# Three of nine score blocks of every pair are copied, negated, from PSUM to SBUF by the pass that takes their row maximum

## The chip, the cores and the metric

One program on one core of a Trainium2 chip. The metric is device time in microseconds. Three runs of the kernel before took 596.67 to 598.54 us, with a median of 598.43 us. The profile comes from one more execution, which took 597.25 us in all and spans 594.6 us from its first to its last instruction.

## The reference

The kernel computes an attention with a threshold on the scores, and passes its output through a soft mixture of experts. All is fp32.

```python
scores = scale * np.matmul(q, k.transpose(0, 1, 3, 2))      # 8 batches, 8 heads, 576 x 576, head size 64
thresh = np.max(scores, axis=-1, keepdims=True) - tau
scores = np.where(scores >= thresh, scores, -1000000000.0)
scores = scores - np.max(scores, axis=-1, keepdims=True)
attn = np.exp(scores)
attn = attn / (np.sum(attn, axis=-1, keepdims=True) + 1e-09)
x = np.matmul(attn, v)                                       # laid out as 4608 tokens x 512
...
logits = x @ phi                                             # 32 slots, 4 for each of 8 experts
# softmax over tokens (d) and over slots (c)
slot_input = d.T @ x
h = np.maximum(slot_input[e] @ w1[e], 0.0)
slot_out[e] = h @ w2[e]
out = c @ slot_out
```

For a row of scores only three things are needed: its maximum, the exponentials of the scores less the maximum, and the sum of those whose score reaches the maximum less tau.

## The kernel before

**Pairs and blocks.** Two heads of a batch make a pair; there are 32 pairs, four to a batch. The 2 x 576 rows of scores of a pair are nine blocks of 128 rows by 576 keys (`i` = 0 to 8 in `pair`): four from each head, and a ninth that holds the last 64 rows of both heads (its probabilities are the buffer `pL`, those of the others lie two by two in four buffers `p2`).

**The steps of a block.** TensorE (PE) computes the scores into a PSUM region `s` (L500, for the ninth block L505). VectorE (DVE) takes the negated row maximum, `nmx` (L510). ScalarE (ACT) writes exp(s + nmx) to SBUF (L518). GpSimd (POOL) makes the threshold `thr` = -nmx - |tau| (L521). DVE reads the scores a second time, compares them with `thr`, multiplies the result onto the exponentials and sums the row into `r` (L524): the masked sum. After every two blocks POOL adds 1e-9 to the sums (L531), DVE takes the reciprocals (L534), and POOL scales the two blocks (L538). PE transposes them through PSUM (L425), ACT copies the transposes to SBUF (L430), and PE multiplies them with the values (L585, twice a pair: AVa and AVb). At the end of a batch, `dispatch` updates the mixture's running softmax.

**Four PSUM regions.** All of PSUM is cut into four regions of two banks. A score block takes one whole region, from its matmul until both its readers, the exp and the masked sum, are done. The same four regions serve the transposes, the products with the values and the small work of `dispatch`.

**What sets the order.** `G.add` only records an operation with an engine, a duration in ns for the planner, a due time, and what it reads and writes. `Order.plan` then lays all operations of the attention part out in one go: each engine takes, whenever it is free in the planner's own clock, the due operation with the lowest number for which buffers can be had. The due times come from `TABLE`, one number for each operation of the first pair, of every middle pair, of the last pair, and of the ends of batches. On the chip each engine then runs its list strictly in that order.

**Weights.** The 64 units of expert weights (512 KB each) go to SBUF: 28 (`NPRE`) during the attention part into slots of their own, 19 (`NHOST`) into the space that the last pairs of the attention leave, and 17 into slots that the first expert products have used up. After the last pair come the expert products (L880, L914) and the combination with the output (L954 to L974).

Of the kernel before, what the change touches and what calls it, by code (L numbers as in the profile page):

```python
# [1054 lines left out]
```

## Time and profile before

| What | us |
|---|---|
| Median of three runs | 598.43 |
| The profiled execution, in all | 597.25 |
| Its span | 594.6 |
| Steady rhythm of the pairs, from | about 23 |
| Two batches (eight pairs and their two ends), steady | 126.83 |
| One pair, steady | 14.97 |
| Last product of the attention part with the values, end | about 520 |
| Expert products, last end | about 563 |

The granted clock of TensorE is 1.00 in all stretches up to 580 us. The profile has a page with totals of each engine, groups of instructions by line, a view of the waits, a chain of the work that ended last, a timeline of each engine, and windows that give each engine's busy time in a stretch. A duration in these views is that of the instruction by itself; DVE starts the next a little before the last ends, so the cost of one in a row of them is read from the distance of two starts in the timeline.

### The profile page before, as it was taken

Reading aid. Unit: us, or ns where it says so; the run is one execution under the profiler, and the core shown is the slowest. Engines: PE = TensorE matmul, PEld = TensorE weight load, DVE = VectorE, ACT = ScalarE, POOL = GpSimd, SP = SyncE. Lnnn points to the kernel's source line nnn. Section 1 sums busy time; section 2 is a strip of 40 time slices with the busy share of each in tenths; the row PEclk is TensorE's granted clock in tenths of the full one; section 3 lists DMA queues with packets and bytes.
Section 4 is the critical chain, followed back from the end, with each engine's and each line's share of the span. In section 5 each row is a group of like instructions: output and inputs, shape, how many; then the busy total and the mean of one; then the engine's idle time right before and its main releaser. Section 6 shows DMA issues by size and latency. Waiting matters only on the chain.

```text
span 594.6 us, 17473 instructions
## 1 busy us (share of the span) xinstructions
PE 544.4 (92%) x6404; PEld 333.5 (56%) x6404; DVE 484.1 (81%) x1146; ACT 442.8 (74%) x753; POOL 348.9 (59%) x799
## 2 busy tenths in 40 slices
PE   8799999999999999999999999999999998999991
PEld 6455555555555555555565555555565555553471
DVE  5999998999898998999889989998989999431182
ACT  3788887888888887888878888888788887622071
POOL 2877776577676775677657765776667755511030
PEclk9999999999999999999999999999999999999996
DMA  7255555355543554533333332333223322699578
GB/s 164 66 154 153 156 154 153 86 156 154 153 132 115 154 154 133 154 83 84 83 84 84 84 84 70 81 81 82 56 70 83 81 64 60 239 361 408 233 309 325
DMA packets 31988, 82.97 MB, mean 140 GB/s; under 512 B 4640, under 2 KB 12832, under 8 KB 31904
## 3 DMA queue, kind: packets, MB, share of 16 engines
q1 hardware_dynamic: 31904, 81.87, 45.7%
q8 instruction: 50, 0.82, 0.6%
q14 instruction: 34, 0.28, 0.2%
HBM read 72.42 MB, written 9.44 MB: 138 GB/s over the span
## 4 chain that ended last, share of the span: by engine, by line
PE 54%; ACT 20%; DVE 9%; issue 8%; POOL 5%; DMA 1%; DVEq 0%; POOLq 0%; ACTq 0%
PE ps L585 22%; PE ps L500 10%; PE ps L425 10%; ACT p L518 6%; ACT pTb L430 5%; DVE p L524 4%; ACT pTa L430 4%; POOL p L538 3%; ACT pTl L430 3%; PE h L880 3%; DVE nmx L510 2%; PE so L914 2%; ACT pTl L570 1%; PE ps L720 1%; PE ps L417 1%
## 5 line engine op out<-in xcount | busy, mean ns | idle before, releaser
L510 DVE TENSOR_REDUCE nmx<-ps 128x1 f32<-128x576 f32 x288 | 205.5, 752 | 30.3 <-PE ps L500 26.7
L518 ACT ACTIVATE p<-ps,nmx 128x576 f32<-128x576 f32 x256 | 183.5, 746 | 29.4 <-DVE nmx L510 25.2
L538 POOL TENSOR_SCALAR p<-p,ri 128x576 f32<-128x576 f32 x256 | 188.1, 742 | 24.2 <-PE ps L500 13.5
L524 DVE SCALAR_TENSOR_TENSOR p<-ps,thr,p 128x576 f32<-128x576 f32 x256 | 199.7, 811 | 2.9 <-POOL thr L521 2.7
L500 PE MATMUL ps<-k,q 64*128 64x288 f32 x1024 | 168.7, 432 | 2.9 <-DVE p L524 1.5
L425 PE MATMUL ps<-ident,p 64*128 64x64 f32 x2304 | 105.9, 227 | 24.2 <-POOL thr L521 10.3
L425 PEld LDWEIGHTS ps<-ident,p 64*128 64x128 f32 x2304 | 88.3, 138 | 55.1 <-POOL thr L521 14.1
L500 PEld LDWEIGHTS ps<-k,q 64*128 64x128 f32 x1024 | 84.5, 187 | 36.6 <-ACT pTb L430 11.8
L521 POOL TENSOR_SCALAR thr<-nmx,nabs 128x1 f32<-128x1 f32 x288 | 75.1, 264 | 37.2 <-DVE nmx L510 27.5
L531 POOL TENSOR_SCALAR ri<-r 128x2 f32<-128x2 f32 (+1 forms) x160 | 30.6, 192 | 95.9 <-DVE p L524 41.8
L430 ACT COPY pTb<-ps 128x1024 f32<-128x1024 f32 (+1 forms) x95 | 80.7, 878 | 2.0 <-PE ps L425 0.9
L585 PE MATMUL ps<-pTb,vv 128*64 128x320 f32 x512 | 75.9, 438 | 1.3
L430 ACT COPY pTa<-ps 128x1024 f32<-128x1024 f32 x64 | 65.4, 1024 | 8.6 <-PE ps L425 7.7
L585 PE MATMUL ps<-pTa,vv 128*64 128x256 f32 x512 | 62.3, 385 | 0.0
L430 ACT COPY xT<-ps 128x256 f32<-128x256 f32 (+1 forms) x63 | 25.1, 399 | 46.7 <-PE ps L585 46.7
L585 PEld LDWEIGHTS ps<-pTb,vv 128*64 128x64 f32 x512 | 34.0, 136 | 39.0 <-ACT pTb L430 13.6
L585 PEld LDWEIGHTS ps<-pTa,vv 128*64 128x64 f32 x512 | 33.9, 136 | 25.8 <-ACT pTa L430 11.5
L585 PE MATMUL ps<-pTl,vv 128*64 128x256 f32 (+1 forms) x256 | 41.9, 406 | 0.0
L534 DVE RECIPROCAL ri<-ri 128x2 f32<-128x2 f32 (+1 forms) x160 | 25.9, 162 | 14.2 <-POOL ri L531 14.1
L845 POOL TENSOR_TENSOR c<-lall,crow 128x512 f32<-128x512 f32 x9 | 9.3, 1043 | 44.1 <-PE ct L417 39.1
L430 ACT COPY pTl<-ps 128x256 f32<-128x256 f32 x64 | 23.7, 370 | 6.2 <-PE ps L425 5.6
L524 DVE SCALAR_TENSOR_TENSOR pL<-ps,thr,pL 128x576 f32<-128x576 f32 x32 | 26.0, 814 | 0.7 <-ACT pL L518 0.7
(126 smaller groups left out, 493.2 us busy)
## 6 DMA issues: line engine op xcount, KB each, us to landing
w<-in_w SPq DMA_DIRECT2D x45, 512.0 KB, 6.8
q<-in_qT SPq DMA_DIRECT2D x62, 288.0 KB, 4.6
vv<-in_vt SPq DMA_DIRECT2D x32, 320.0 KB, 3.0
host<-in_w SPq DMA_DIRECT2D x19, 512.0 KB, 6.3
k<-in_kT SPq DMA_DIRECT2D x62, 144.0 KB, 3.1
out<-w SPq DMA_DIRECT2D x11, 512.0 KB, 3.7
out<-host SPq DMA_DIRECT2D x5, 512.0 KB, 5.0
out<-host SPq DMA_DIRECT2D x4, 256.0 KB, 4.5
```

What stands on the lines that cost most here:

```text
L425: nc.tensor.transpose(out=s[:, g, c:c + 64], in_=ins[g], identity=ident[rows[g], rows[g]], tile_position=(64 * g, 0))
L430: G.add("ACT", 51 + 0.833 * n, nom, lambda: nc.scalar.copy(*io()), r, w)
L500: nc.tensor.matmul(s.t[:, g, 0:HS], qt.t[rows[g], h, c * 128:(c + 1) * 128], kt.t[rows[g], h * HS:(h + 1) * HS], start=True, stop=True, ti ...
L510: dve(665, t + OFF['mx'], [s], [nmx], lambda s=s, nmx=nmx: nc.vector.tensor_reduce(out=nmx.t, in_=s.t[:, :, 0:HS], axis=AX.XY, op=ALU.max, ...
L518: G.add("ACT", 624, t + OFF['ex'], lambda s=s, nmx=nmx, view=view: nc.scalar.activation(view().rearrange("p (a k) -> p a k", a=2), s.t[:, ...
L521: pool(250, t + OFF['th'], lambda nmx=nmx, thr=thr: nc.gpsimd.tensor_scalar(out=thr.t, in0=nmx.t, scalar1=-1.0, scalar2=nabs, op0=ALU.mult ...
L524: lambda s=s, thr=thr, view=view, i=i: nc.vector.scalar_tensor_tensor(out=view().rearrange("p (a k) -> p a k", a=2), in0=s.t[:, :, 0:HS], ...
L531: pool(200, t + OFF['ri'], lambda e=e: nc.gpsimd.tensor_scalar(out=ri.t[:, e], in0=r.t[:, e], scalar1=1e-9, scalar2=1.0, op0=ALU.add, op1= ...
L534: dve(84, t + OFF['ri'], [], [ri[c]], lambda e=e: nc.vector.reciprocal(ri.t[:, e], ri.t[:, e]))
L538: pool(725, t + OFF['sc'], lambda k=k, view=view_: nc.gpsimd.tensor_scalar(out=view(), in0=view(), scalar1=ri.t[:, k:k + 1], **one), [ri[c ...
L585: nc.tensor.matmul(lone(w)[h * 64:(h + 1) * 64, 0:n], vv.t[:, v0:v0 + 64], p0, start=(kb == 0), stop=(kb == 4), tile_position=(0, h * 64), ...
L880: nc.tensor.matmul(hp[n][g * 32:(g + 1) * 32, :], siT[:, kb, :], t[g][:, n * 512:(n + 1) * 512], start=(kb == 0), stop=(kb == 3), tile_pos ...
```

## The change

For the blocks `i` = 3, 7 and 8 of every pair (`AWAY`) the pass that takes the maximum is another instruction: a tensor_scalar that multiplies the scores by -1, writes all 576 columns to a new SBUF buffer `ss`, and accumulates the row minimum of what it wrote, which is `nmx`. The exp then reads `ss` with scale -1, the threshold is `nmx` + |tau| (`pabs`, made once at the start), and the masked sum compares `ss` with "less or equal". The PSUM region of these blocks is thus free after the first pass. The planner books 729 ns for the new pass (665 for the old one) and 950 ns for the masked sum of these blocks (729 for the others).

Two buffers `ss` take 2 x 2304 bytes of each partition, so two weight slots fewer are loaded ahead (`NPRE` 26) and one more goes to the space left by the last pairs (`NHOST` 20). The whole `TABLE` of due times has new numbers.

```diff
 SLOTS = dict(
-    xT=5, x=1, xl=1, ll=1, d=1, M=2, f=2, dl=1,
+    ss=2, xT=5, x=1, xl=1, ll=1, d=1, M=2, f=2, dl=1,
...
+AWAY = (3, 7, 8)
-NPRE = 28
+NPRE = 26
-NHOST = 19
+NHOST = 20
...
     ("pair", [
-        -39.07, 7.16, -6.00, -18.55, 45.67, 1.80, -6.99, -30.08, -3.44, -30.97, 2.08, 68.99, -30.85, 31.25,
+        -72.86, -63.55, -108.61, 6.81, -58.86, -2.91, 27.83, -59.96, -44.75, -2.50, -3.18, 1.99, -50.60, -50.58,
...
+    pabs = cp.tile([128, 1], F32, name="pabs")
+    nc.vector.tensor_scalar(out=pabs, in0=nabs, scalar1=-1.0, scalar2=None, op0=ALU.mult)
...
-            dve(665, t + OFF['mx'], [s], [nmx], lambda s=s, nmx=nmx: nc.vector.tensor_reduce(
-                out=nmx.t, in_=s.t[:, :, 0:HS], axis=AX.XY, op=ALU.max, negate=True))
+            away = i in AWAY
+            ss = Buf("ss") if away else s
+            if away:
+                dve(729, t + OFF['mx'], [s], [ss, nmx], lambda s=s, ss=ss, nmx=nmx: nc.vector.tensor_scalar(
+                    out=ss.t.rearrange("p (a k) -> p a k", a=2), in0=s.t[:, :, 0:HS], scalar1=-1.0, scalar2=3.4028234663852886e38,
+                    op0=ALU.mult, op1=ALU.min, accum_out=nmx.t))
+            else:
+                dve(665, t + OFF['mx'], [s], [nmx], lambda s=s, nmx=nmx: nc.vector.tensor_reduce(
+                    out=nmx.t, in_=s.t[:, :, 0:HS], axis=AX.XY, op=ALU.max, negate=True))
...
-                view().rearrange("p (a k) -> p a k", a=2), s.t[:, :, 0:HS], AF.Exp, bias=nmx.t),
-                [s, nmx], [dst])
+                view().rearrange("p (a k) -> p a k", a=2), sv(), AF.Exp, bias=nmx.t, scale=-1.0 if away else 1.0),
+                [ss, nmx], [dst])
...
-            dve(729, t + OFF['st'], [s, thr], [dst, r[i]],
+            dve(950 if away else 729, t + OFF['st'], [ss, thr], [dst, r[i]],
...
-                    op0=ALU.is_ge, op1=ALU.mult, accum_out=r.t[:, i:i + 1]))
+                    op0=ALU.is_le if away else ALU.is_ge, op1=ALU.mult, accum_out=r.t[:, i:i + 1]))
```

**Order, first place: DVE, the first passes of a steady pair.** In the rows below, `nmx` is written by the first pass and `r` by the masked sum; the names `ps_221` to `ps_224` are the four PSUM regions in the kernel before, `ps_223` to `ps_226` in the changed one; of the probabilities, two blocks share each `p_` buffer. Line numbers of the changed kernel are larger: its first pass is L522 or, to SBUF, L518, its masked sum L538, its reciprocal L548. Before, from one masked sum to the next group's first:

```order
L524 SCALAR_TENSOR_TENSOR p_175,r_153<-ps_221,thr_165,p_175 128x576
L534 RECIPROCAL ri_155<-ri_155 128x2
L510 TENSOR_REDUCE nmx_158<-ps_224 128x1
L510 TENSOR_REDUCE nmx_159<-ps_223 128x1
L510 TENSOR_REDUCE nmx_160<-ps_221 128x1
L524 SCALAR_TENSOR_TENSOR p_175,r_153<-ps_224,thr_162,p_175 128x576
L524 SCALAR_TENSOR_TENSOR p_173,r_153<-ps_223,thr_163,p_173 128x576
L524 SCALAR_TENSOR_TENSOR p_173,r_153<-ps_221,thr_164,p_173 128x576
```

And in the changed kernel, at the fourth block of a pair:

```order
L538 SCALAR_TENSOR_TENSOR p_178,r_155<-ps_226,thr_165,p_178 128x576
L518 TENSOR_SCALAR ss_173,nmx_162<-ps_223 128x576
L548 RECIPROCAL ri_158<-ri_158 128x2
L522 TENSOR_REDUCE nmx_163<-ps_226 128x1
L522 TENSOR_REDUCE nmx_160<-ps_225 128x1
L522 TENSOR_REDUCE nmx_161<-ps_223 128x1
L538 SCALAR_TENSOR_TENSOR p_177,r_155<-ss_173,thr_166,p_177 128x576
L538 SCALAR_TENSOR_TENSOR p_179,r_155<-ps_226,thr_167,p_179 128x576
```

Before, three first passes alternate with three masked sums. Now the fourth block's first pass frees region `ps_223`, which the third of the next three first passes already reads with other scores, while the fourth block's masked sum is still to come.

**Second place: DVE and POOL at the eighth and ninth block.** DVE in the changed kernel, from the eighth block's first pass on:

```order
L518 TENSOR_SCALAR ss_172,nmx_162<-ps_223 128x576
L548 RECIPROCAL ri_158<-ri_158 128x2
L518 TENSOR_SCALAR ss_173,nmx_163<-ps_225 128x576
L538 SCALAR_TENSOR_TENSOR p_180,r_155<-ss_172,thr_166,p_180 128x576
L522 TENSOR_REDUCE nmx_160<-ps_223 128x1
L548 RECIPROCAL ri_158<-ri_158 128x2
L522 TENSOR_REDUCE nmx_161<-ps_226 128x1
L538 SCALAR_TENSOR_TENSOR pL_168,r_155<-ss_173,thr_167,pL_168 128x576
```

POOL over the same stretch, where L534 is the threshold, L545 the sum plus 1e-9, and L552 the scaling:

```order
L534 TENSOR_SCALAR thr_166<-nmx_162,pabs 128x1
L552 TENSOR_SCALAR p_179<-p_179,ri_158 128x576
L534 TENSOR_SCALAR thr_167<-nmx_163,pabs 128x1
L552 TENSOR_SCALAR p_179<-p_179,ri_158 128x576
L545 TENSOR_SCALAR ri_158<-r_155 128x2
L534 TENSOR_SCALAR thr_165<-nmx_160,nabs 128x1
L552 TENSOR_SCALAR p_180<-p_180,ri_158 128x576 x2
```

The two masked sums that read `ss` stand beside four scalings of POOL; the second reciprocal of DVE here needs POOL's `ri_158<-r_155`, which stands behind the second scaling of `p_179`.

**Third place: PE at the fourth block.** Before, in the stretch from the transposes of the third pair of blocks to the product AVa (L585):

```order
L425 MATMUL ps_223<-ident,p_174 128x64 x16
L425 MATMUL ps_222<-ident,p_173 128x64 x16
L500 MATMUL ps_224<-k_180,q_181 128x288 x2
L500 MATMUL ps_223<-k_180,q_181 128x288 x2
L500 MATMUL ps_221<-k_180,q_181 128x288 x2
L585 MATMUL ps_222<-pTa_167,vv_187 64x256 x8
```

In the changed kernel, from AVa (L599) on:

```order
L599 MATMUL ps_223<-pTa_169,vv_191 64x256 x8
L429 MATMUL ps_225<-ident,p_180 128x64 x16
L504 MATMUL ps_223<-k_184,q_185 128x288 x2
L429 MATMUL ps_224<-ident,pL_168 128x64 x10
L504 MATMUL ps_226<-k_184,q_185 128x288 x2
L504 MATMUL ps_225<-k_184,q_185 128x288 x2
L504 MATMUL ps_223<-k_184,q_185 128x288 x2
L599 MATMUL ps_224<-pTb_170,vv_191 64x320 x8
```

Where PE computed three blocks of scores in a row, each time when three regions had come free, it now computes the fourth block by itself, ahead of the transposes of `pL`, and refills its region two score blocks later.

More of the change, by code (lines that the diff above doesn't have):

```diff
@@ L36 @@
     ("first", [
[7 rows of a table removed]
[7 rows of a table added]
     ]),
     ("pair", [
[7 rows of a table removed]
[7 rows of a table added]
     ]),
     ("last", [
[7 rows of a table removed]
[7 rows of a table added]
     ]),
     ("even", [
-        16.52, 28.06, 40.62, 2.54, 18.66, -25.55, -10.72, 7.36, 8.07, -2.18, -70.04, 14.73, -23.47, -5.39,
-        -37.78, 8.58, -52.36, 3.09, -21.09, -131.89, -170.48,
+        -30.47, -37.06, 24.60, 30.08, 7.26, -35.11, 16.79, 83.50, -32.39, -35.06, 17.14, -34.56, 17.93, -32.11,
+        19.53, -4.10, -31.88, -12.38, 11.69, -86.72, -40.06,
     ]),
     ("odd", [
-        17.10, -172.20, 18.00, 26.05, 43.42, 15.85, -172.33, -174.86, 19.63, -186.95, 22.45, 7.15, 40.94, -176.55,
-        7.29, -183.72, -7.12, -183.57, -7.76, 18.18, -19.92, -7.94, -113.51,
+        -24.46, -3.27, 69.87, -9.59, 69.74, 5.50, -108.05, -108.31, -38.46, -0.12, -2.54, -4.13, 19.43, -4.06,
+        -33.14, -41.70, -40.96, -56.16, 84.84, -13.33, -20.97, -59.83, -36.88,
     ]),
     ("end", [
[3 rows of a table removed]
[3 rows of a table added]
     ]),
     ("soft", [
-        100.90, 91.42, 61.67, 67.57, 81.87, 103.44,
+        152.74, 197.65, -28.19, 198.68, 150.14, -35.62,
     ]),
@@ L357, in softmax_attention_soft_moe @@
         pTa=([128, 2, 4, QA], F32), pTb=([128, 2, 4, S - QA], F32), pTl=([128, S], F32), l4=([128, S], F32),
-        xT=([128, S], F32), x=([128, 4, DM], F32), xl=([128, DM], F32), ll=([128, 4, NS], F32),
+        ss=([128, S], F32), xT=([128, S], F32), x=([128, 4, DM], F32), xl=([128, DM], F32), ll=([128, 4, NS], F32),
         d=([128, 4, NS], F32), M=([128, 2], F32), f=([128, 1], F32), dl=([128, 4, NS], F32),
     )
-    levels = (("k0", "q0", "vv0"), ("k1", "q1"), ("p2",), ("pL", "pTa", "pTb", "pTl", "vv1", "r", "ri", "nmx", "thr"))
+    levels = (("k0", "q0", "vv0"), ("k1", "q1"), ("p2",), ("pL", "pTa", "pTb", "pTl", "vv1", "r", "ri", "nmx", "thr", "ss"))
     level = {k: i for i, ks in enumerate(levels) for k in ks}
@@ L509, in pair @@
                   mode=HALVES if i < 8 else QUADS)
-            dve(665, t + OFF['mx'], [s], [nmx], lambda s=s, nmx=nmx: nc.vector.tensor_reduce(
-                out=nmx.t, in_=s.t[:, :, 0:HS], axis=AX.XY, op=ALU.max, negate=True))
+            away = i in AWAY
[7 more added lines that the diff above has]
+                    out=nmx.t, in_=s.t[:, :, 0:HS], axis=AX.XY, op=ALU.max, negate=True))
+            sv = (lambda ss=ss: ss.t.rearrange("p (a k) -> p a k", a=2)) if away else (lambda s=s: s.t[:, :, 0:HS])
             if i == 8:
@@ L517, in pair @@
                 dst, view = p2s[c][h], (lambda c=c, h=h: p2s[c].t[:, h * S:(h + 1) * S])
-            G.add("ACT", 624, t + OFF['ex'], lambda s=s, nmx=nmx, view=view: nc.scalar.activation(
-                view().rearrange("p (a k) -> p a k", a=2), s.t[:, :, 0:HS], AF.Exp, bias=nmx.t),
-                [s, nmx], [dst])
-            pool(250, t + OFF['th'], lambda nmx=nmx, thr=thr: nc.gpsimd.tensor_scalar(
-                out=thr.t, in0=nmx.t, scalar1=-1.0, scalar2=nabs, op0=ALU.mult, op1=ALU.add), [nmx], [thr])
-            dve(729, t + OFF['st'], [s, thr], [dst, r[i]],
-                lambda s=s, thr=thr, view=view, i=i: nc.vector.scalar_tensor_tensor(
-                    out=view().rearrange("p (a k) -> p a k", a=2), in0=s.t[:, :, 0:HS],
+            G.add("ACT", 624, t + OFF['ex'], lambda sv=sv, nmx=nmx, view=view, away=away: nc.scalar.activation(
+                view().rearrange("p (a k) -> p a k", a=2), sv(), AF.Exp, bias=nmx.t, scale=-1.0 if away else 1.0),
+                [ss, nmx], [dst])
+            pool(250, t + OFF['th'], lambda nmx=nmx, thr=thr, away=away: nc.gpsimd.tensor_scalar(
+                out=thr.t, in0=nmx.t, scalar1=1.0 if away else -1.0, scalar2=pabs if away else nabs, op0=ALU.mult,
+                op1=ALU.add), [nmx], [thr])
+            dve(950 if away else 729, t + OFF['st'], [ss, thr], [dst, r[i]],
+                lambda sv=sv, thr=thr, view=view, i=i, away=away: nc.vector.scalar_tensor_tensor(
+                    out=view().rearrange("p (a k) -> p a k", a=2), in0=sv(),
                     scalar=thr.t, in1=view().rearrange("p (a k) -> p a k", a=2),
-                    op0=ALU.is_ge, op1=ALU.mult, accum_out=r.t[:, i:i + 1]))
+                    op0=ALU.is_le if away else ALU.is_ge, op1=ALU.mult, accum_out=r.t[:, i:i + 1]))
             if h == 1 or i == 8:
```

46 rows, old and new, of the table TABLE are left out of this document.

## The prediction

> **What bounds the kernel now.** I read the page's totals first, then windows over steady pairs, then the timelines of DVE and PE in one pair, then the waits.
>
> ```profile
> span 594.6 us, 17473 instructions
> PE 544.4 (92%) x6404; PEld 333.5 (56%) x6404; DVE 484.1 (81%) x1146; ACT 442.8 (74%) x753; POOL 348.9 (59%) x799
> ...
> 321.74:448.57 126.83, 118.92 (x1480) 73.62 (x1480) 113.60 (x272) 105.35 (x180) 84.75 (x194) 1.00 0.31 79
> 321.74:336.71 14.97, 14.03 (x170) 8.82 (x170) 13.54 (x33) 12.62 (x22) 10.52 (x24) 1.00 0.32 78
> ```
>
> The windows give the length of a stretch, then the busy time of PE, weight loads, DVE, ACT and POOL. A steady pair takes 14.97 us; PE is busy for 14.03 of it, DVE for 13.54, POOL for 10.52. No engine is full, but two are nearly so: PE has 0.94 us to give, DVE 1.43. They wait for each other, as DVE's timeline in that pair shows (start, length, what; in brackets the idle time before it and what ended that).
>
> ```profile
> 322.54 2.09 DVE L510 TENSOR_REDUCE nmx<-ps 128x1 f32<-128x576 f32 x3
> 324.54 0.81 DVE L524 SCALAR_TENSOR_TENSOR p<-ps,thr,p 128x576 f32<-128x576 f32 x1
> ...
> 325.28 0.81 DVE L524 SCALAR_TENSOR_TENSOR p<-ps,thr,p 128x576 f32<-128x576 f32 x1
> ...
> 327.15 0.17 DVE L534 RECIPROCAL ri<-ri 128x2 f32<-128x2 f32 x1 [0.23 <-POOL ri L531]
> 327.52 2.09 DVE L510 TENSOR_REDUCE nmx<-ps 128x1 f32<-128x576 f32 x3 [0.20 <-PE ps L500]
> ...
> 332.95 2.23 DVE L510 TENSOR_REDUCE nmx<-ps 128x1 f32<-128x576 f32 x3 [0.66 <-PE ps L500]
> ```
>
> Three first passes start within 2.00 us (322.54 to 324.54), so one costs 0.67; a masked sum costs 0.74 (324.54 to 325.28), its 811 ns less the overlap. The first passes then stand still for scores: a region is free only after its masked sum, PE needs time to refill it, and meanwhile DVE has nothing to read. PE waits in turn for probabilities:
>
> ```profile
> 335.02 0.71 PE L425 MATMUL ps<-ident,p 64*128 64x64 f32 x16 [0.61 <-POOL thr L521]
> 335.98 0.71 PE L425 MATMUL ps<-ident,p 64*128 64x64 f32 x16 [0.24 <-DVE p L524]
> ```
>
> Over the whole run the view of the waits shows what DVE loses so:
>
> ```profile
> DVE nmx L510 <- PE ps L500: 26.7, 57, 2.6
> DVE ri L534 <- POOL ri L531: 14.1, 55, 0.6
> ```
>
> Over 32 pairs that is 0.83 us a pair for scores and 0.44 for the sums from POOL. The first is what earlier free regions can remove. The second can go by the order alone: before, a reciprocal follows directly on the masked sum whose row sums POOL has yet to pass on (first place of the order); in the changed kernel a first pass of 0.7 us stands between, more than POOL's 0.19 for L531 (below) and the 0.23 that DVE now waits.
>
> **The change, part by part.** All terms are for one steady pair.
>
> *The new first pass* reads the same 128x576 from PSUM. No such row exists before. Its nearest rows:
>
> ```profile
> L510 DVE TENSOR_REDUCE nmx<-ps 128x1 f32<-128x576 f32 x288 | 205.5, 752 | 30.3 <-PE ps L500 26.7 <-PE ps L505 0.2
> L524 DVE SCALAR_TENSOR_TENSOR p<-ps,thr,p 128x576 f32<-128x576 f32 x256 | 199.7, 811 | 2.9 <-POOL thr L521 2.7 <-ACT p L518 0.2
> L524 DVE DVE_READ_ACCUMULATOR p<-ps,thr,p 128x1 f32 x256 | 21.3, 83 | 0.0
> ```
>
> It writes a full tile and reads an accumulator out, as the masked sum does, so it should cost 0.74 in place of 0.67. That is 3 x 0.07 = +0.2 us. The bounds are the reduce (0) and both parts one behind the other, 811 + 83 less 670 (+0.22 each, +0.7).
>
> *The exp from SBUF.* ACT rows with an SBUF source:
>
> ```profile
> L518 ACT ACTIVATE p<-ps,nmx 128x576 f32<-128x576 f32 x256 | 183.5, 746 | 29.4 <-DVE nmx L510 25.2 <-DVE ri L534 3.3 <-PE ps L425 0.2
> L696 ACT ACTIVATE d<-d 128x128 f32<-128x128 f32 x8 | 2.5, 312 | 1.0 <-DVE d L694 0.5
> L763 ACT ACTIVATE lall<-lall 128x992 f32<-128x992 f32 x1 | 1.1, 1052 | 0.0
> ```
>
> A line through the two SBUF rows (312 at 128 columns, 1052 at 992) gives 696 ns at 576, no more than the 746 from PSUM. I take 0; ACT is idle for 2.35 us a pair (14.97 less 12.62), which also covers 0.1 either way. The threshold keeps its form, and `pabs` is one instruction of the start.
>
> *The masked sum from SBUF* is the term that decides. It now has both tensors in SBUF. One row of this form exists, at 32 columns, and one with PSUM at a single column:
>
> ```profile
> L733 DVE SCALAR_TENSOR_TENSOR csum<-csum,f,ps 128x1 f32<-128x1 f32 x7 | 1.5, 209 | 0.0
> L706 DVE SCALAR_TENSOR_TENSOR msel<-msel,ones,st 128x32 f32<-128x32 f32 x1 | 0.2, 246 | 0.0
> L761 DVE TENSOR_TENSOR lall<-lall,crow 128x992 f32<-128x992 f32 x1 | 1.2, 1185 | 0.0
> ```
>
> From 1 column (209) to 576 (811) a column costs 1.05 ns, so 32 columns should take 242; measured are 246. By itself the instruction is as fast as from PSUM. The same holds for L761, two SBUF inputs, at 1185 ns for 992 columns. The Trainium skill says otherwise on its page "Vector Engine (DVE) Microarchitecture Reference", section "Points that are easy to get wrong": this family of instructions with two SBUF sources that are not bf16 runs at half the rate. By that rule L706 would need some 275 ns; the trace speaks against it, at this small size.
>
> What no row shows is such an instruction beside a busy POOL. Both L761 and L706 ran while POOL stood idle:
>
> ```profile
> 486.86 1.19 DVE L761 TENSOR_TENSOR lall<-lall,crow 128x992 f32<-128x992 f32 x1
> ...
> 488.87 0.19 POOL L531 TENSOR_SCALAR ri<-r 128x2 f32<-128x2 f32 x1 [2.38 <-DVE p L524]
> ...
> 526.11 0.25 DVE L706 SCALAR_TENSOR_TENSOR msel<-msel,ones,st 128x32 f32<-128x32 f32 x1
> ...
> 528.43 1.04 POOL L845 TENSOR_TENSOR c<-lall,crow 128x512 f32<-128x512 f32 x1 [4.97 <-PE ps L725]
> ...
> L538 POOL TENSOR_SCALAR p<-p,ri 128x576 f32<-128x576 f32 x256 | 188.1, 742 | 24.2 <-PE ps L500 13.5 <-DVE ri L534 6.3 <-PE ps L425 0.6
> L521 POOL TENSOR_SCALAR thr<-nmx,nabs 128x1 f32<-128x1 f32 x288 | 75.1, 264 | 37.2 <-DVE nmx L510 27.5 <-DVE ri L534 4.0 <-POOL thr L521 3.0
> ```
>
> So the cost x of one is bounded below by 0.74 (no mutual wait) and above by 0.74 + 0.74 = 1.48 (each stands behind a whole scaling of POOL). I take 0.95, by POOL's occupancy: nine scalings and one of the keys at 0.74 fill 7.4 of 14.97 us, the rest of its 10.52 is small work. One that arrives at random meets a scaling half the time, with half of it left: 0.18, plus some 0.03 for the small ones. The diff's own duration for the planner is 950 too, but that is no measurement. The three places in the order agree with a mixed case: the fourth block's sum comes when POOL makes thresholds, the eighth's and ninth's beside scalings of `p_179` and `p_180`.
>
> The Trainium skill has this as a rule ("SBUF — State Buffer", section "Who interferes with whom"): a DVE instruction with two SBUF inputs contends with a GpSimd instruction that reads SBUF, and the later one waits for the whole of the other. No run here shows it yet. By it a wait at each of the three places would come out near my 0.2 on average, and POOL would be held as well.
>
> *Sum for DVE.* 13.54 less three masked sums (2.21) plus 0.2 is 11.53; with 3 x 0.95 it is 14.38. To that come waits that remain of the 1.43: some for scores, and the reciprocal behind the eighth block, whose `ri` POOL makes after a scaling. I allow 0.2, which gives **14.6 us a pair**. PE needs 14.03 and has the same work and mode changes as before, so it fits, with 0.57 to spare in place of 0.94.
>
> *What takes the place of the stall.* With the wait for scores gone, DVE itself is next: it would be 98% busy. Behind each of its instructions stand the thresholds and sums of POOL, and behind these the transposes of PE. The gain is 14.97 less 14.6, 0.37 us, times 31 pairs: 11.5 us. The ends of the batches have the same extra work as before (126.83 less 8 x 14.97 is 7.1 for two); I count no gain there.
>
> *Start and end.* In the first and the last pair DVE works alone for long stretches, so that the added 3 x 0.21 + 0.2 = 0.8 shows in full in both: +1.6. One weight unit more comes after the attention (18 for 17), and one more in the last pairs' space. The transfers end between 550 and 570, the last units are used from 561 on:
>
> ```profile
> 532.41 17.82 SPq L407 DMA_DIRECT2D w<-in_w x17
> ...
> 550.00:560.00 10.00, 10.00 (x96) 3.54 (x88) 1.29 (x2) 0.00 (x0) 0.00 (x0) 1.00 0.87 346
> 560.00:570.00 10.00, 9.81 (x73) 7.11 (x66) 4.21 (x7) 4.35 (x9) 1.04 (x1) 1.00 0.20 84
> ...
> 561.02 1.05 PE L914 MATMUL h00e<-w,hz 128*32 128x256 f32 x16
> ```
>
> A unit takes 512 KB / 400 GB/s = 1.3 us. At 87% busy the DMA finishes about 1.3 us before 560, so some 2.5 us of cover face two units of 2.6: about +0.5.
>
> The sum is 597.25 - 11.5 + 1.6 + 0.5 = 587.9, made against the profiled execution, which lies 1.2 under the median of the runs: **588 us**, a gain of 1.7%.
>
> **The rivals.**
>
> *No mutual wait* (x = 0.74): DVE needs 13.74, PE 14.03 becomes the bound, with some 0.2 of waits 14.2 a pair. 597.25 - 31 x 0.77 + 0.9 is 574. For it: both engines' durations are even, today. Against: nothing of this form has run beside POOL. Chance 0.15.
>
> *One stall for another* (597): the score wait goes, but PE meets POOL's scalings later (the 0.61 above) and the rhythm stays at 14.97. For it: PE has only 0.94 to give. Against: DVE's idle time is twice as much for scores as for sums. Chance 0.13.
>
> *Slower: POOL and the masked sums from `ss` hold each other.* The place is the eighth and ninth block: the sum waits behind a scaling of `p_179`, POOL's next operations wait behind the sum, and DVE's next reciprocal needs POOL's `ri`, queued behind the second scaling. It decides from 11.53 + 3x + 0.2 = 14.97 on, that is x = 1.08, a wait of 0.34 or half a scaling. At x = 1.2, with 0.3 us for the late reciprocal, a pair takes 15.4 or 15.5: 31 x 0.48 is 15, plus 2.5 at the ends, 614. Against: the average wait of 0.21 lies under 0.34. Chance 0.21.
>
> *Half rate of the masked sum* (x = 1.34): 15.75 a pair, 31 x 0.78 and 4 at the ends, 625. L706 speaks against it. Chance 0.05. It is what the first of the two pages above would give.
>
> **How the numbers follow.** The forecast (581 to 595, from x = 0.88 to 1.02 and the bounds of the first pass) has 0.46, no mutual wait 0.15, one stall for another 0.13, slower by mutual holding 0.21, half rate 0.05. Faster by over 0.3% (what a measurement of this kernel can tell from no change) is 0.46 + 0.15 = 0.61, within it 0.13, slower 0.26. The range from 575 to 610 leaves out the lower half of the first rival (0.08) and the part of the slower cases above 610 (0.12). It is 588 and not a mean of the cases, since the forecast is the likeliest.
>
> **What would show it right or wrong.** In the profile of the changed kernel: the group of new first passes near 811 ns with an accumulator read behind each; the wait of first passes for L504 down from 26.7 us to under 10; the masked sums from `ss` in a spread between 811 and some 1500 ns, against an even 811 for the others; DVE over 95% busy in a steady pair; a pair at 14.6. If their rows are an even 811, the first rival holds and PE is the bound; if their mean lies over 1100, or POOL's scalings have grown from 742 by more than 200, the slower one does. A tail longer than 563 less the attention's gain would show the weights late.

## The result, and the profile after

Four runs of the changed kernel took 603.37 to 605.99 us, with a median of 604.41 us, against 598.48 us for the kernel before on the same chip. The ratio is 1.010, with a 95% interval from 1.008 to 1.013: **slower by 1.0%**. The forecast was 588 us. The profiled execution took 605.17 us, with a span of 603.4.

The page of the changed kernel: totals of each engine, then the groups (busy us, mean ns of one, and the idle time before them with what ended it).

```profile
span 603.4 us, 17397 instructions
PE 547.3 (91%) x6404; PEld 340.5 (56%) x6404; DVE 488.8 (81%) x1243; ACT 447.7 (74%) x753; POOL 392.9 (65%) x799
...
L552 POOL TENSOR_SCALAR p<-p,ri 128x576 f32<-128x576 f32 x256 | 203.1, 798 | 19.9 <-DVE ri L548 12.7
...
L538 DVE SCALAR_TENSOR_TENSOR p<-ps,thr,p 128x576 f32<-128x576 f32 x192 | 151.8, 810 | 9.3 <-ACT p L531 4.4
...
L534 POOL TENSOR_SCALAR thr<-nmx,nabs 128x1 f32<-128x1 f32 x192 | 67.5, 352 | 33.9 <-DVE nmx L522 18.2
...
L518 DVE TENSOR_SCALAR_CACHE_REDUCE ss<-ps 128x576 f32<-128x576 f32 x96 | 72.2, 752 | 15.3 <-PE ps L504 9.8
...
L534 POOL TENSOR_SCALAR thr<-nmx,pabs 128x1 f32<-128x1 f32 x96 | 37.4, 389 | 41.9 <-DVE ri L548 34.7
...
L538 DVE SCALAR_TENSOR_TENSOR p<-ss,thr,p 128x576 f32<-128x576 f32 x64 | 53.2, 831 | 4.0 <-ACT p L531 2.6
L531 ACT ACTIVATE p<-ss,nmx 128x576 f32<-128x576 f32 x64 | 49.7, 777 | 6.3 <-DVE ss L518 6.3
```

POOL's program is the same as before, 799 instructions of the same forms, yet it is busy for 392.9 us instead of 348.9. The thresholds, two groups now, make up 29.8 of these 44.0 us (67.5 + 37.4 - 75.1), the scalings of `p` 15.0 (203.1 - 188.1). DVE grew by 4.7 us only. The view of single lines gives the spread (shortest, median and longest in ns):

```profile
L534 POOL TENSOR_SCALAR thr<-nmx,pabs x96: 263/266/1114, 13.8 to 515.9; 128x1 f32<-128x1 f32 x96
L552 POOL TENSOR_SCALAR p<-p,ri x256: 733/746/1357, 16.0 to 517.7; 128x576 f32<-128x576 f32 x128
L538 DVE SCALAR_TENSOR_TENSOR p<-ps,thr,p x192: 791/812/820, 9.2 to 513.0; 128x576 f32<-128x576 f32 x192
L538 DVE SCALAR_TENSOR_TENSOR p<-ss,thr,p x64: 799/816/1345, 14.1 to 510.9; 128x576 f32<-128x576 f32 x64
L538 DVE SCALAR_TENSOR_TENSOR pL<-ss,thr,pL x32: 798/928/1379, 23.3 to 517.1; 128x576 f32<-128x576 f32 x32
```

The medians of POOL are those of before, and some of its instructions take 0.5 us and more on top: they stand still. The shortest masked sum from `ss` takes 799 ns, about as long as one from PSUM (791 to 820). The waits show both halves of the result:

```profile
PEld ps L429 <- POOL p L552: 23.7, 19, 1.5
PE ps L429 <- POOL p L552: 14.9, 18, 1.0
DVE ri L548 <- POOL ri L545: 13.9, 31, 0.9
DVE ss L518 <- PE ps L504: 9.8, 21, 0.8
DVE nmx L522 <- PE ps L504: 9.3, 15, 2.3
```

The first passes wait 19.1 us for scores (9.8 + 9.3) where they waited 26.7: that stall did shrink. In its place TensorE waits for POOL's scalings: 23.7 us of its weight loads' waits bear that name, where 7.6 did before. The windows of one pair inside a batch and of two batches (length, then busy time of PE, weight loads, DVE, ACT and POOL; the third number from the end is the granted clock of TensorE):

```profile
315.23:330.45 15.22, 13.80 (x170) 8.75 (x171) 13.72 (x36) 12.90 (x22) 11.96 (x25) 1.00 0.31 81
300.01:428.06 128.05, 119.58 (x1480) 75.53 (x1480) 114.16 (x296) 106.66 (x180) 95.77 (x195) 0.99 0.30 78
```

A pair inside a batch takes 15.22 us instead of 14.97. PE is busy in it for 0.2 us less than before, DVE for 0.2 more and POOL for 1.4 more. The two batches take 128.05 us instead of 126.83, but their clock is 0.99: for 3.4 us of them TensorE was granted half of it, and the pair with that stretch in it took 16.70 us. The two batches before these have no such stretch:

```profile
172.86:300.01 127.15, 118.47 (x1481) 74.44 (x1481) 114.20 (x296) 106.54 (x180) 95.92 (x195) 1.00 0.42 111
391.70:395.10 3.40, 3.40 (x28) 2.58 (x26) 1.97 (x6) 2.41 (x6) 1.65 (x4) 0.50 0.00 0
```

The same pairs, the tenth to the seventeenth, take 127.29 us in the kernel before (169.14 to 296.43). So the steady rhythm neither won nor lost: what pairs inside a batch lose, the ends of the batches give back.

The 8.8 us by which the spans differ (603.4 less 594.6) gather at single places. Both kernels start their first AVb at 29.9 us. The changed one is 3.4 us behind at the ninth (156.34 against 152.97), 4.4 at the 25th, 5.4 at the last, 7.6 at its end and 8.8 at the end of the program. Three half-clock stretches have a large part in that: by my estimate 1.1 us at 105 (16.38 us for a pair that takes 15.23 in other batches), 1.5 at 391.7 (16.70 against 15.22), and 2.2 at the end of the attention, where the last AVb runs at a granted clock of 0.50 to 0.57. It takes 4.54 us; in the kernel before, whose row comes first, it took 2.32:

```profile
516.96 2.32 PE L585 MATMUL ps<-pTb,vv 128*64 128x320 f32 x16
```

```profile
519.03 0.71 PE L429 MATMUL ps<-ident,p 64*128 64x64 f32 x16 [1.02 <-POOL p L552]
...
522.36 4.54 PE L599 MATMUL ps<-pTb,vv 128*64 128x320 f32 x16 [1.36 <-DVE pTb L438]
```

```profile
521.00:524.00 3.00, 1.64 (x6) 0.77 (x8) 0.83 (x2) 0.91 (x4) 0.00 (x0) 0.57 0.62 167
524.00:527.00 3.00, 3.00 (x14) 1.42 (x12) 0.00 (x0) 0.00 (x0) 0.00 (x0) 0.50 0.92 359
```

The profile before has none of these three: its clock is 1.00 up to 580 us. The four executions of the changed kernel were granted 0.977 to 0.984 of the clock over their whole span, the profiled one the least; those of the kernel before, in the later runs, 0.984 to 0.994. The other 4 us of the difference were not traced to one place.

**How a pair gets longer.** POOL's timeline around the eighth block's masked sum (start, length, what; idle time before in brackets):

```profile
302.88 1.47 POOL L552 TENSOR_SCALAR p<-p,ri 128x576 f32<-128x576 f32 x2 [0.59 <-DVE ri L548]
...
305.45 0.27 POOL L534 TENSOR_SCALAR thr<-nmx,pabs 128x1 f32<-128x1 f32 x1 [0.82 <-DVE ri L548]
305.68 0.75 POOL L552 TENSOR_SCALAR p<-p,ri 128x576 f32<-128x576 f32 x1
306.41 0.75 POOL L534 TENSOR_SCALAR thr<-nmx,pabs 128x1 f32<-128x1 f32 x1
307.13 0.74 POOL L552 TENSOR_SCALAR p<-p,ri 128x576 f32<-128x576 f32 x1
307.96 0.19 POOL L545 TENSOR_SCALAR ri<-r 128x2 f32<-128x2 f32 x1
...
308.52 1.96 POOL L552 TENSOR_SCALAR p<-p,ri 128x576 f32<-128x576 f32 x2
```

And DVE and PE in the same stretch:

```profile
306.18 0.85 DVE L538 SCALAR_TENSOR_TENSOR p<-ss,thr,p 128x576 f32<-128x576 f32 x1 [0.17 <-ACT p L531]
...
308.19 0.17 DVE L548 RECIPROCAL ri<-ri 128x2 f32<-128x2 f32 x1 [0.48 <-POOL ri L545]
...
308.94 0.93 DVE L538 SCALAR_TENSOR_TENSOR pL<-ss,thr,pL 128x576 f32<-128x576 f32 x1
```

```profile
310.54 0.71 PE L429 MATMUL ps<-ident,p 64*128 64x64 f32 x16 [0.84 <-POOL p L552]
```

The threshold at 306.41 needs 0.27 us by itself; it takes 0.75 because the eighth block's masked sum has been running since 306.18. Behind it on POOL stand a scaling and the `ri` for which DVE's reciprocal waits (0.48). That reciprocal releases two scalings, which take 1.96 instead of 1.47 because the ninth block's masked sum starts beside them. PE stands still for the second of them (0.84). The two delays, 0.48 and 0.49 us, are in series: POOL, DVE, POOL, PE. That is the reading to be tested.

### The profile page after: what moved, and what is told of

It is laid out like the page before. It is cut to its first block, busy times and chain, and to the rows that moved or that the text cites. A ratio compares the mean times of both kernels' runs of the same rounds, so it can differ in the third digit from the quotient of the medians.

```text
span 603.4 us, 17397 instructions
## 1 busy us (share of the span) xinstructions
PE 547.3 (91%) x6404; PEld 340.5 (56%) x6404; DVE 488.8 (81%) x1243; ACT 447.7 (74%) x753; POOL 392.9 (65%) x799
## 4 chain that ended last, share of the span: by engine, by line
PE 22%; DVE 11%; POOL 10%; issue 6%; DMA 5%; ACT 4%; DVEq 0%; POOLq 0%; SPq 0%; ACTq 0%
PE ps L599 8%; POOL p L552 5%; DVE p L538 5%; PE ps L504 5%; DMA w<-in_w 5%; PE ps L429 4%; POOL thr L534 3%; DVE nmx L522 2%; DVE ss L518 1%; PE ps L664 1%; ACT p L531 1%; ACT pTb L434 1%; PE ps L421 1%; DMA out<-w 1%; POOL pL L552 1%
## 5 line engine op out<-in xcount | busy, mean ns | idle before, releaser
L552 POOL TENSOR_SCALAR p<-p,ri 128x576 f32<-128x576 f32 x256 | 203.1, 798 | 19.9 <-DVE ri L548 12.7
L531 ACT ACTIVATE p<-ps,nmx 128x576 f32<-128x576 f32 x192 | 135.1, 742 | 33.3 <-DVE nmx L522 28.9
L538 DVE SCALAR_TENSOR_TENSOR p<-ps,thr,p 128x576 f32<-128x576 f32 x192 | 151.8, 810 | 9.3 <-ACT p L531 4.4
L522 DVE TENSOR_REDUCE nmx<-ps 128x1 f32<-128x576 f32 x192 | 138.7, 750 | 12.3 <-PE ps L504 9.3
L429 PEld LDWEIGHTS ps<-ident,p 64*128 64x128 f32 x2304 | 87.2, 139 | 71.7 <-POOL p L552 23.7
L504 PEld LDWEIGHTS ps<-k,q 64*128 64x128 f32 x1024 | 91.9, 190 | 23.6 <-DVE p L538 6.0
L534 POOL TENSOR_SCALAR thr<-nmx,nabs 128x1 f32<-128x1 f32 x192 | 67.5, 352 | 33.9 <-DVE nmx L522 18.2
L518 DVE TENSOR_SCALAR_CACHE_REDUCE ss<-ps 128x576 f32<-128x576 f32 x96 | 72.2, 752 | 15.3 <-PE ps L504 9.8
L599 PE MATMUL ps<-pTb,vv 128*64 128x320 f32 x512 | 78.1, 448 | 2.7 <-DVE pTb L438 1.4
L534 POOL TENSOR_SCALAR thr<-nmx,pabs 128x1 f32<-128x1 f32 x96 | 37.4, 389 | 41.9 <-DVE ri L548 34.7
L599 PE MATMUL ps<-pTa,vv 128*64 128x256 f32 x512 | 62.5, 386 | 0.8
L599 PEld LDWEIGHTS ps<-pTb,vv 128*64 128x64 f32 x512 | 34.6, 139 | 39.3 <-ACT pTb L434 11.4
L538 DVE SCALAR_TENSOR_TENSOR p<-ss,thr,p 128x576 f32<-128x576 f32 x64 | 53.2, 831 | 4.0 <-ACT p L531 2.6
L531 ACT ACTIVATE p<-ss,nmx 128x576 f32<-128x576 f32 x64 | 49.7, 777 | 6.3 <-DVE ss L518 6.3
L599 PEld LDWEIGHTS ps<-pTa,vv 128*64 128x64 f32 x512 | 34.0, 137 | 28.7 <-ACT pTa L434 7.7
L545 POOL TENSOR_SCALAR ri<-r 128x2 f32<-128x2 f32 (+1 forms) x160 | 31.3, 196 | 27.4 <-DVE p L538 12.3
L599 PE MATMUL ps<-pTl,vv 128*64 128x256 f32 (+1 forms) x256 | 42.5, 410 | 0.0
```

The costliest lines, as they stand in the source:

```text
L429: nc.tensor.transpose(out=s[:, g, c:c + 64], in_=ins[g], identity=ident[rows[g], rows[g]], tile_position=(64 * g, 0))
L504: nc.tensor.matmul(s.t[:, g, 0:HS], qt.t[rows[g], h, c * 128:(c + 1) * 128], kt.t[rows[g], h * HS:(h + 1) * HS], start=True, stop=True, ti ...
L518: dve(729, t + OFF['mx'], [s], [ss, nmx], lambda s=s, ss=ss, nmx=nmx: nc.vector.tensor_scalar(out=ss.t.rearrange("p (a k) -> p a k", a=2), ...
L522: dve(665, t + OFF['mx'], [s], [nmx], lambda s=s, nmx=nmx: nc.vector.tensor_reduce(out=nmx.t, in_=s.t[:, :, 0:HS], axis=AX.XY, op=ALU.max, ...
L531: G.add("ACT", 624, t + OFF['ex'], lambda sv=sv, nmx=nmx, view=view, away=away: nc.scalar.activation(view().rearrange("p (a k) -> p a k", ...
L534: pool(250, t + OFF['th'], lambda nmx=nmx, thr=thr, away=away: nc.gpsimd.tensor_scalar(out=thr.t, in0=nmx.t, scalar1=1.0 if away else -1.0 ...
```

## The experiments

Three theories stood at the start. **Theory 1**: the price comes from masked sums with two SBUF inputs, which stop POOL. **Theory 2**: it comes from the new order, which makes PE wait for POOL's scalings anyway. **Theory 3**: it comes from the half-clock stretches of TensorE.

**One input instead of two (e1).** The masked sum of blocks 3, 7 and 8 reads `ss` alone, so that the exponentials of these blocks are left out of the result; order, regions and weights stay as changed.

```diff
-                lambda ...: nc.vector.scalar_tensor_tensor(
+                lambda ...: nc.vector.tensor_scalar(
+                    out=view()..., in0=sv(), scalar1=thr.t, scalar2=0.0,
+                    op0=ALU.is_le, op1=ALU.add, accum_out=r.t[:, i:i + 1]) if away else nc.vector.scalar_tensor_tensor(
```

> The changed kernel in its own order, but the masked sum of the three blocks reads only the copied scores: it compares, writes 0 or 1 over the exponentials and sums that (it leaves the exponentials of these blocks out). It has one SBUF tensor input in place of two; length, order, buffers and dependencies stay. Theory 1 (the masked sums with two SBUF inputs and POOL's instructions hold each other; POOL's busy time rose from 348.9 to 392.9 us by that, and its late results stop PE): POOL busy falls back to 347 to 352 us, no scaling over 800 ns, and the time falls to 583 to 592 us. Theory 2 (the new order by itself is worse, the mutual wait is only seen beside it): POOL busy falls as well, but the time stays at 600 to 606. Theory 3 (half-clock episodes of TensorE make the difference: mean granted clock 0.977 against 0.991): the time follows the clock, some 600 if the clock is back at 0.99 and nothing else changes.

Measured: 583.62 us (582.56 to 584.63), ratio to before 0.977 (0.974 to 0.979). From its groups, and its windows of one pair and of the tenth to the seventeenth pair:

```profile
L554 POOL TENSOR_SCALAR p<-p,ri 128x576 f32<-128x576 f32 x256 | 189.8, 746 | 23.5 <-DVE ri L550 15.0 <-DVE M L701 3.1 <-PE ps L601 2.8
L538 DVE TENSOR_SCALAR_CACHE_REDUCE p<-ss,thr 128x576 f32<-128x576 f32 x64 | 51.7, 807 | 5.1 <-ACT p L531 3.2 <-POOL thr L534 0.7 <-POOL p L554 0.5
L534 POOL TENSOR_SCALAR thr<-nmx,nabs 128x1 f32<-128x1 f32 x192 | 51.2, 267 | 33.4 <-DVE nmx L522 14.7 <-DVE ri L550 13.4
L534 POOL TENSOR_SCALAR thr<-nmx,pabs 128x1 f32<-128x1 f32 x96 | 26.5, 276 | 42.5 <-DVE ri L550 35.4 <-DVE ss L518 6.7 <-POOL p L554 0.3
```

```profile
305.25:319.71 14.46, 13.73 (x171) 8.74 (x171) 13.48 (x36) 12.79 (x22) 10.58 (x25) 1.00 0.31 86
167.54:290.79 123.25, 118.02 (x1480) 74.20 (x1481) 112.92 (x296) 106.02 (x180) 85.17 (x195) 1.00 0.42 115
```

In the pair shown PE waits at one place, at the transposes of the eighth block again, now for POOL's `ri`:

```profile
315.50 1.21 PE L429 MATMUL ps<-ident,p 64*128 64x64 f32 x32 [0.56 <-POOL ri L547]
```

The new form is no faster (794 ns at the shortest, against 799 for the old form), and POOL is back near its old durations. The second input costs 20.8 us (604.4 less 583.6). Theory 2 falls: the same order is 14.4 us faster than before (598.01 in these runs) when POOL is not stopped.

Theory 3 alone falls too: it gave some 600 us, and the gain shows where the clock is full. Two batches without a half-clock stretch take 123.25 us instead of 127.15, and four times 3.9 is 15.6 of the 20.8 us. The rest is about what the three stretches cost above (4.8 us). None of the three is left here: the clock is 1.00 from 26 to 540 us. Whether the stops of POOL bring such stretches about was not tried by itself; they went together.

**The same parts in the old order.** Three kernels keep the order of before, with the changed kernel's weight counts and two fixed buffers `ss`. The first (e4) has only the new first pass, which writes an `ss` that nobody reads:

```diff
-                dve(665, t + OFF['mx'], [s], [nmx], ... nc.vector.tensor_reduce(
+                dve(665, t + OFF['mx'], [s], [nmx], ... nc.vector.tensor_scalar(
+                    out=ssv(), in0=s.t[:, :, 0:HS], scalar1=-1.0, ... accum_out=nmx.t))
-NPRE = 28
+NPRE = 26
-NHOST = 19
+NHOST = 20
```

> The kernel before in its old order, with the weight slots of the change (26 and 20) and the new first pass of the three blocks; its copy is read by nobody, exp and masked sum still read PSUM. All theories: POOL unchanged at 349 us. DVE busy rises by 3 x 32 x (0 to 0.2) us; the time is 598 to 606, where 600 to 602 is my estimate from 0.07 us for each (6 us of DVE work, of which some fills idle time).

Measured: 598.74 us, ratio 1.0015 (0.9998 to 1.0031). Copy and weight slots together cost 0.3% at most.

The second (e5) has the whole change but the order, so that the exp and the masked sum read `ss` as well:

> The whole change (copy, exp and masked sum from SBUF, weight slots) in the old order of instructions of every engine. Theory 1: POOL busy rises to 375 to 400 us here too, and the time is 602 to 615, over the copy alone by 2 to 10. Theory 2 (the order is what lost): the time is at or under that of the copy alone, 594 to 602, since regions come free earlier.

Measured: 605.45 us, ratio 1.0136 (1.0114 to 1.0158). The third (e6) is the second with the one-input masked sum of e1:

> As the one before, with one SBUF input in the masked sums of the three blocks (their exponentials are left out). Theory 1: POOL busy 349 us, the time 2 to 12 us under the whole change in the old order. Theory 2: no more than 2 us under it.

Measured: 600.5 us, ratio 1.005 (1.0033 to 1.0068). So the second input costs 5.0 us in the old order and 20.8 in the new one, though POOL is held for comparable times: its busy time falls by 33.6 us from the second kernel to the third (382.6 to 349.0) and by 41.5 in the new order (392.9 to 351.4). In the old order thresholds are held, not scalings, and DVE's own sums of the ninth block, which take 1112 ns in the mean:

```profile
L550 POOL TENSOR_SCALAR p<-p,ri 128x576 f32<-128x576 f32 x256 | 189.9, 749 | 23.2 <-PE ps L503 13.5 <-DVE ri L546 5.9
L532 POOL TENSOR_SCALAR thr<-nmx,nabs 128x1 f32<-128x1 f32 x192 | 77.1, 402 | 24.4 <-DVE nmx L520 13.6 <-POOL thr L532 3.9 <-DVE ri L546 3.7
L536 DVE SCALAR_TENSOR_TENSOR pL<-ss,thr,pL 128x576 f32<-128x576 f32 x32 | 35.6, 1112 | 0.3 <-ACT pL L529 0.3
```

These rows are of the second kernel, where DVE is busy for 12.2 us more than in the third (498.5 to 486.3). And freed regions without the new order bring nothing: the third kernel is not below the first.

**Which of the three masked sums pays.** If every held instruction cost alike, each block would have a third of the price; if what counts is what stands behind it, block 3 should cost little and block 8 most. The edit is that of e1, for one block at a time: block 3 (below), block 7, block 8.

```diff
-  ... if away else nc.vector.scalar_tensor_tensor(
+  ... if i in (3,) else nc.vector.scalar_tensor_tensor(
```

> The changed kernel, but the masked sum of block 3 alone reads only the copied scores (one SBUF input); its exponentials are left out of the result, those of blocks 7 and 8 are not. One input at all three blocks was worth 20.8 us (604.4 to 583.6). Theory L, the price depends on what the held GpSimd instruction stands ahead of: block 3's masked sum holds two 128x1 thresholds (1.04 us instead of 0.53 at 300.97 us), behind which GpSimd has 0.59 us of slack before the next scaling; worth 0 to 4 us, 600.5 to 604.5 us. Theory C, every lock costs the same: a third of 20.8, 6.9 us, 597.5 us. Both: thresholds shorter by some 10 to 20 us in sum, scalings hardly.

> The changed kernel, but the masked sum of block 7 alone reads only the copied scores (one SBUF input); its exponentials are left out of the result, those of blocks 3 and 8 are not. Theory L: its masked sum holds one threshold (0.75 instead of 0.27 us at 306.41 us), whose scaling behind it feeds the reciprocal chain of the last pair of blocks; worth 2 to 7 us, 597.5 to 602.5 us. Theory C: 597.5 us.

> The changed kernel, but the masked sum of block 8 alone reads only the copied scores (one SBUF input); its exponentials are left out of the result, those of blocks 3 and 7 are not. Theory L: its masked sum holds the two scalings for which TensorE's transposes wait (1.96 instead of 1.47 us at 308.52 us, then 0.84 us of TensorE waiting for p); worth 10 to 18 us, 586 to 594 us, and TensorE's wait for p of the scaling line falls by half or more. Theory C: 597.5 us.

| One input at | us | gain on the changed kernel, us | POOL busy, us | tenth to seventeenth pair, us |
|---|---|---|---|---|
| no block (the changed kernel) | 604.41 | | 392.9 | 127.15 |
| block 3 | 603.76 | 0.6 | 380.4 | 127.20 |
| block 7 | 594.73 | 9.7 | 381.9 | 125.76 |
| block 8 | 590.43 | 14.0 | 377.3 | 124.44 |
| all three | 583.62 | 20.8 | 351.4 | 123.25 |

POOL is held for 11 to 16 us less each time, but the gains are 0.6, 9.7 and 14.0 us: what a stop costs is decided by its place. The last column, two batches at a clock of 1.00, says so without the half-clock stretches: 0, 1.4 and 2.7 us, or 0, 5.6 and 10.8 for the whole attention. The gains of blocks 7 and 8 have 3 to 4 us beyond that, which is near what the stretches cost: those at 105 and 391.7 us are in the profile of block 3's kernel too, and missing in the other two. Block 7 was expected at 2 to 7 us; its 5.6 in the rhythm lie in that range, the 9.7 of the whole do not. The rows that recover are those of the reading above, the thresholds of the copied blocks without block 7's second input, the scalings without block 8's:

```profile
L534 POOL TENSOR_SCALAR thr<-nmx,pabs 128x1 f32<-128x1 f32 x96 | 26.5, 276 | 40.8 <-DVE ri L550 33.7 <-DVE ss L518 6.7 <-POOL p L554 0.2
```

```profile
L554 POOL TENSOR_SCALAR p<-p,ri 128x576 f32<-128x576 f32 x256 | 190.3, 748 | 19.8 <-DVE ri L550 12.7 <-PE ps L601 2.4 <-DVE M L701 2.3
```

The three gains sum to 24.3 us, over the 20.8 of all together; in the rhythm 4.1 us face 3.9, so most of the excess lies in the stretches, which went with either of the two edits. The form of the instruction is no cause either: at block 3 it changed too, for 0.6 us. One part of the expectation for block 8 held only by the letter: the wait of the transposes' weight loads that bears the scalings' name fell from 23.7 to 9.1 us, but 14.2 us now bear the name of a threshold, where 6.5 did.

**A way round (g1).** If a scaling held at this place is the cost, it helps to take one off POOL there. ACT is idle at 309 us. The scaling of block 7 goes to ACT at the same place of the order, and all is computed:

```diff
+                    if k in (7,):
+                        pool(725, t + OFF['sc'], lambda k=k, view=view_: nc.scalar.activation(
+                            view(), view(), AF.Copy, scale=ri.t[:, k:k + 1]), [ri[c]], [dst_])
+                        continue
                     pool(725, t + OFF['sc'], lambda k=k, view=view_: nc.gpsimd.tensor_scalar(
```

> The changed kernel with the scaling of block 7 moved from GpSimd to ScalarE (activation Copy with ri as scale), at the same place of the order; all is computed. 32 scalings of 0.80 us leave GpSimd, at the place where TensorE's transposes wait for them, and stand in a gap of ScalarE (0.56 us of idle before the next exponential at 309.12 us). Theory L: the transposes start some 0.7 us earlier in each pair, and the threshold behind the scaling too; 0.3 to 0.6 us for each of the 32 pairs, 585 to 595 us, faster than both kernels. Rival, ScalarE's exponentials come later by the 0.7 us and the pair stays at 15.2 us: 602 to 606 us.

Measured: 592.97 us (592.3 to 593.47), ratio to before 0.990 (0.988 to 0.992): **faster than both kernels**, by 5.7 us (598.66 in these runs) and by 11.4 us. A pair inside a batch, and, in another pair, PE at the place of the 0.84 us:

```profile
434.05:449.00 14.95, 13.87 (x171) 8.82 (x171) 13.60 (x36) 13.25 (x23) 11.27 (x24) 1.00 0.31 84
```

```profile
304.75 0.71 PE L429 MATMUL ps<-ident,p 64*128 64x64 f32 x16 [0.57 <-POOL ri L545]
305.80 0.71 PE L429 MATMUL ps<-ident,p 64*128 64x64 f32 x16 [0.34 <-DVE p L538]
```

The pair is as long as in the kernel before (14.97). The gain on that kernel lies at the ends of the batches: the tenth to the seventeenth pair take 124.96 us, where they took 127.29 before and 127.15 in the changed kernel.

The same move in the kernel before is the control (g2):

> The kernel before with the same move as in g1: the scaling of block 7 goes from GpSimd to ScalarE, nothing else. If g1's 12 us over the changed kernel were only the gain of less work on GpSimd, whatever the order, the kernel before would gain as much: 586 to 590 us. Theory L, the move pays where a held scaling stands ahead of TensorE's transposes, and before no masked sum has two SBUF inputs: within 4 us of before, 595 to 602 us.

Measured: 599.04 us, ratio 1.0003 (0.9988 to 1.0018), although POOL's busy time falls there too, to 327.2 us. Less work for POOL was worth something only where TensorE waited for it.

**Two that failed (g3, g4).** In g1 thresholds are still held (192 of them at a mean of 419 ns). So in g3 block 2's was given to DVE, and in g4 all of them:

```diff
-            pool(250, ..., lambda nmx=nmx, thr=thr, away=away: nc.gpsimd.tensor_scalar(
+            pool(250, ..., lambda nmx=nmx, thr=thr, away=away, e=nc.vector if i in (2,) else nc.gpsimd: e.tensor_scalar(
```

> g1 with the threshold of block 2 (a 128x1 instruction) computed on VectorE instead of GpSimd; all is computed. In g1 this threshold is held behind the ninth block's masked sum in every second pass (0.75 instead of 0.27 us at 303.72 us) and TensorE waits 19.4 us in all for thresholds. Theory L: half of that wait to all of it goes, 575 to 588 us. Rival, VectorE takes over what GpSimd loses (some 32 x 0.1 us) and the wait moves to the next scaling: 591 to 595 us.

Measured: 600.83 us, ratio 1.006 (1.004 to 1.008), worse than either expectation. DVE's timeline after the ninth block's masked sum, and PE's second group of transposes there:

```profile
305.83 0.93 DVE L538 SCALAR_TENSOR_TENSOR pL<-ss,thr,pL 128x576 f32<-128x576 f32 x1
...
307.36 0.20 DVE L534 TENSOR_SCALAR thr<-nmx,nabs 128x1 f32<-128x1 f32 x1
307.66 0.82 DVE L538 SCALAR_TENSOR_TENSOR p<-ps,thr,p 128x576 f32<-128x576 f32 x1
```

```profile
308.54 0.71 PE L429 MATMUL ps<-ident,p 64*128 64x64 f32 x16 [0.65 <-DVE p L538]
```

From threshold to masked sum 0.30 us pass on DVE, and the masked sum is what releases PE's second group of transposes. PE's wait for it rose from 0.34 to 0.65 us, and a pair inside a batch from 14.95 to 15.25. The tenth to the seventeenth pair take 125.92 us instead of 124.96, so the rhythm accounts for some 3.8 of the 7.9 us lost. Two half-clock stretches in this profile, at 324.7 and 389.6, which g1's does not have, took 1.5 us each. What the threshold had cost on POOL did not outweigh its cost on DVE.

> g1 with all 288 thresholds on VectorE instead of GpSimd; all is computed. GpSimd loses 118 us of busy time (80.3 + 37.7 in g1), VectorE gains 288 small instructions; by the nearest row, the reciprocal's 0.16 us, with much of it overlapped, 0.07 to 0.16 us each, 20 to 46 us on an engine that is 82% busy. Theory L (GpSimd's held instructions set the pair): 575 to 592 us. Rival, VectorE becomes the bound: 595 to 620 us.

Measured: 605.34 us, ratio 1.013 (1.009 to 1.016). POOL's busy time falls from 371.2 to 265.1 us and DVE's rises from 488.0 to 519.2. The time is that of the rival, and its reading, that DVE becomes the bound, fits: DVE is busy for 121.7 of the 127.3 us of the tenth to the seventeenth pair.

## Why the prediction was wrong

**The step that failed** is the cost of the masked sum from `ss`, 0.95 us "by POOL's occupancy", put wholly on DVE as a mean wait. On DVE it was too high: in the stretch shown DVE goes on 0.78 us after the start of the eighth block's sum, and the whole run lost 4.3 us there (64 times 21 ns and 32 times 93 over the 810 of those from PSUM). What I left out of the sum is the other side. The text says that "POOL would be held as well", but no term carries it. It was 44 us of POOL's time, ten times DVE's share, and two of the three stops stand in series ahead of PE's transposes. So a pair inside a batch took 15.22 us and not the 14.6 of the forecast; with these stops taken away it took 14.46.

Two more terms were put at nothing. No gain was counted at the ends of the batches; there the changed order gave back what the pairs lost, so that two batches at full clock take 127.15 us against 127.29. And the sum has no term for TensorE's clock, which had been full through the attention before; half-clock stretches make some 4.8 of the 8.8 us in this profile, by the estimate above. What sets them off stays open.

**Right in the forecast.** The new first pass costs no more than was taken: 752 ns, as long as a reduce (750), where some 811 were forecast, with the accumulator read behind each, and no measurable loss in the kernel with the copy alone. The stall for scores shrank (26.7 to 19.1 us; "under 10" was too hopeful). The two weight units cost nothing that the copy alone shows. The wait for POOL's sums, which was to go by the order alone, stayed (14.1 us before, 13.9 after); without the second input it is 4.2. The gain behind the change was real: without the second input a pair takes 14.46 us, where 14.6 were forecast with DVE's waits in it, and 14.2 by the rival without mutual wait. That rival's 574 us were 9.6 under the 583.62 of the kernel that comes nearest to it, and these 0.26 us a pair make 8 of them: PE still stands still for 0.56 us at 315.50.

**Wrong in small terms.** The exp from SBUF takes 777 ns against 742 from PSUM (it also has scale -1, and the two were not tried apart); my line through two rows gave 696. DVE now waits 7.0 us in all for exponentials (4.4 and 2.6), where it waited 0.2; whether the 35 ns have a part in that was not tried.

**The rivals.** "One stall for another" (597) described the rhythm best: the wait for scores shrank, PE met POOL's scalings later, and two batches stayed as long as before. It named no stop of POOL for that, though, and with one input the same order gained 3.9 us in two batches. The slower one had the right place, the eighth and ninth block, and the right chain through `ri` to the reciprocal. Its price was on the wrong engine: it asked for x = 1.08 on DVE, and the turn came with x at some 0.79 (0.74 and 4.3 us over 96 sums), through stops of 0.48 and 0.49 us on POOL. So its 614 us were too much, and its test by "POOL's scalings ... grown ... by more than 200" too coarse: they grew by 56 ns in the mean, and the thresholds, which it did not name, by 88 and 125.

The rule of the Trainium skill ("SBUF — State Buffer", section "Who interferes with whom"), that such a DVE instruction and one of GpSimd that reads SBUF exclude each other, is what the trace now shows: a threshold of 0.27 us takes 0.75 behind a masked sum. Which side pays was measured: 44 us on POOL and 4 on DVE in the new order, 33.6 and 12.2 in the old one. The half rate of its page "Vector Engine (DVE) Microarchitecture Reference" ("Points that are easy to get wrong") did not appear at 576 columns either: 799 ns at the shortest with two SBUF sources, 791 with one.

## What to carry to other kernels

When an edit gives an instruction of one engine a second operand in the memory that another engine works from, write a term for each engine, and follow what is queued behind the stopped instruction to the next engine that waits. Stops of about the same total (12.5 and 15.6 us of POOL's time) cost 0.6 us in one place and 14 in another; a mean over the engine's occupancy cannot tell these apart, the order at the place can. If the edit is good but for such a stop, one instruction moved off the stopped engine at that place may be worth more than that stop: here 11.4 us. And before a window is multiplied up to the whole run, look at the granted clock in it and take a second one: here the whole 1.22 us by which one pair of batches was longer lay in a single stretch at half clock.

## What the runs showed of the hardware

- In the new order the stops fell almost wholly on POOL: instructions on 128x1 took up to 1.11 us instead of 0.27, though they move one column. I had expected the costs to be shared. In the old order DVE bore about a quarter (12.2 us against 33.6), most of it in the ninth block's sum.
- An exp of 128x576 took 777 ns from SBUF, with scale -1, and 742 from PSUM, with scale 1.
- A threshold on 128x1 takes 0.20 us on DVE, and the instruction that reads it starts 0.30 us after its start, on the same engine.
- Inside the attention TensorE's granted clock fell to 0.50 for single stretches of 3.4 us, as from 391.70, behind waits of PE of 0.84 and 0.40 us. The same two waits stand at 310.54 and 311.65, where the clock stays at 1.00, so they alone do not set it off; what does was not tried. A pair with such a stretch in it took up to 1.5 us longer.
